# An attention and mixture-of-experts kernel: constant tables reordered, two set-up jobs moved back, due times that vary along the tiles

## The chip, the cores and the metric

One Trainium2 chip, one core of it. The metric is device time in microseconds (us) of one execution; of the kernel before, three runs are shown and their median counts. Engines are named as in the profile: PE (TensorE matmul), PEld (its weight load), DVE (VectorE), ACT (ScalarE), POOL (GpSimd), SP (SyncE, which issues most transfers).

## The reference

Attention over 8 batches, 8 heads, 576 positions of width 64, with a linear distance bias per head and a causal window of 128; then a mixture of experts on the 4608 resulting rows of width 512: each row goes to the one of 8 experts with the largest cosine similarity, passes two matrices (512 to 1024, rectified, 1024 to 512), and is scaled by its gate.

```python
scores = scale * np.matmul(q, k.transpose(0, 1, 3, 2))
bias = slopes[:, None, None] * (-np.abs(rel).astype(np.float32))[None, :, :]
mask = (rel >= 0) & (rel < window)
scores = np.where(mask, scores + bias[None], -1000000000.0)
scores = scores - np.max(scores, axis=-1, keepdims=True)
attn = np.exp(scores)
attn = attn / (np.sum(attn, axis=-1, keepdims=True) + 1e-09)
return np.matmul(attn, v).astype(np.float32)
...
logits = xn @ en.T / tau
expert_idx = np.argmax(logits, axis=1)
...
    h = np.maximum(x[mask] @ w1[e], 0.0)
    out[mask] = gate_w[mask, None] * (h @ w2[e])
```

## The kernel before, in words

**Attention** runs over 36 tiles of 128 rows. A batch has four whole tiles and a rest of 64 rows; the rests of two batches make one "pair" tile. A batch's first tile needs no previous keys. Each tile is done in two half tiles of four heads, numbered u = 0 to 71. A half tile passes these stages, each a job on one engine: scores (PE, L565), for tiles with a previous one a merge (DVE), four maxima with the bias added from `tab_full` or `tab_first` (DVE, L592), exponentials (ACT, L600), a flip, which is a transpose through the identity matrix `ident` (PE, L609), the rounded upper half of the result (ACT, L513), the remainder as lower half (DVE, L516), two masks (POOL, L647 and L660; pair tiles write them into the buffers `tails` and `spread`, which must hold zeros elsewhere), values (PE, L680 and L695), reciprocal and normalisation (DVE, L722 and L728). The values need v as an upper half (ACT, L527) and as a difference (POOL, L535, tile `vo`). A tile's result is split again (ACT L741, POOL L754), squared and summed (ACT L750), transposed by a transfer (SP, L758) and multiplied with the expert vectors (PE, L766).

**Routing** takes the tiles in groups of 8, 8, 8, 6, 4 and 2: DVE, PE, ACT and POOL find each row's expert and its place, and POOL then scatters the group's rows tile by tile to memory sorted by expert (L867, "put"). After the third group the expert with most rows is known; its weights are fetched and split, and its first 384 rows, the "head", are computed beside the last tiles.

**The experts** follow in their own plan, with PE bound by two matrix products per expert.

**The order of the work** is written by a list scheduler, `Plan`, when the kernel is built. Each job has an engine, a guessed duration, predecessors, rings of buffers that it takes, and a due time. It picks, on the engine that can start next, the job with the earliest due time among those that can start within that engine's SLACK of the first. FREE says when each engine is through with the set-up work. A due time was STEP (2500 ns) times u plus one offset per stage from `DUE`. On the chip each engine then works strictly in the order so found, and waits where the chip differs from the guesses. `early` is a start that the plan does not go below; a job with `fill` comes after all others. The scatters are spaced by SPREAD (2600 ns) and, in due time, by `gap` (6600 ns) from one to the next in a group.

**The set-up** stands ahead of the plan and runs in the order written. POOL makes `ident`, `minus`, three parts of `erow`, `ones`, `tri` (L225 to L249), then `rel_full` by iota (L285); DVE makes slopes, `wrap_full`, `tab_full` and two masks from it (L297 to L305); POOL makes `tab_first` by four selects (L312). PE multiplies `ones` with itself ten times as a warm-up (L460), then begins the scores. SP loads k and q of tiles 0 and 1, then the expert vectors (`emb`) and tau. Two jobs on POOL follow as part of the plan: `tables` (iota tables and a zero row for the scatters, L261 to L271) and `tails` (zeros in four buffers of 128x1024, L1010). The expert vectors are normalised and flipped by a chain of 15 small jobs (L490 to L504); `expert11` scales `emb` (L501) and `expert12` flips it.

## Time and profile before

| what | value |
|---|---|
| runs | 595.65, 595.83, 597.27 us; median 595.83 |
| profiled execution | 594.54 us, span 592.7 us |
| busy in the span | PE 558.4, DVE 468.8, ACT 373.3, POOL 332.7 us |
| mean granted clock of PE | 0.985 of full speed |
| weight loads (PEld) | 367.1 us |

The busy time of an engine over the whole span mixes the attention, the join and the experts, which have different limits; stretches have to be read one by one. In a timeline row the number in brackets is how long the engine stood idle before it, and what released it. [...]

### The profile page before, as it was taken

Reading aid. Unit: us, or ns where it says so; the run is one execution under the profiler, and the core shown is the slowest. Engines: PE = TensorE matmul, PEld = TensorE weight load, DVE = VectorE, ACT = ScalarE, POOL = GpSimd, SP = SyncE. Lnnn points to the kernel's source line nnn. Section 1 sums busy time; section 2 is a strip of 40 time slices with the busy share of each in tenths; the row PEclk is TensorE's granted clock in tenths of the full one; section 3 lists DMA queues with packets and bytes.
Section 4 is the critical chain, followed back from the end, with each engine's and each line's share of the span. In section 5 each row is a group of like instructions: output and inputs, shape, how many; then the busy total and the mean of one; then the engine's idle time right before and its main releaser. Section 6 shows DMA issues by size and latency. Waiting matters only on the chain. (4 is left out here: it accounts for less than half of the span.)

```text
span 592.7 us, 16519 instructions
## 1 busy us (share of the span) xinstructions
PE 558.4 (94%) x6097; PEld 367.1 (62%) x6097; DVE 468.8 (79%) x1540; ACT 373.3 (63%) x867; POOL 332.7 (56%) x445
## 2 busy tenths in 40 slices
PE   6899999999989779999999999999999999999995
PEld 3677676776767646465654764764855845754854
DVE  5799898898888778245899986798997998997670
ACT  4799999999999964134554535654744636644320
POOL 7779899999989996312617702614623352332011
PEclk9799999999999969999999999999999999999999
DMA  6589999999899597698767263446376166221001
GB/s 232 164 187 241 242 208 214 261 238 260 223 249 231 145 240 180 201 211 297 182 168 267 107 159 123 144 110 227 112 158 232 36 178 218 78 79 64 15 19 55
DMA packets 117971, 103.05 MB, mean 174 GB/s; under 512 B 85109, under 2 KB 86133, under 8 KB 117888
## 3 DMA queue, kind: packets, MB, share of 16 engines
q1 hardware_dynamic: 112048, 83.05, 55.4%
q0 software_dynamic: 5840, 18.92, 8.8%
q8 instruction: 49, 0.80, 0.6%
q14 instruction: 34, 0.28, 0.2%
HBM read 61.92 MB, written 28.12 MB: 152 GB/s over the span
## 5 line engine op out<-in xcount | busy, mean ns | idle before, releaser
L396 POOL DMA_INDIRECT out_dram<-y,ids x32 | 43.7, 1366 | 134.0 <-ACT y L1581 93.7
L600 ACT ACTIVATE pe<-sb,nm 128x128 f32<-128x128 f32 x288 | 95.3, 402 | 8.9 <-DVE nm L592 8.6
L1568 PE MATMUL ps<-w2h,hh 128*128 128x512 f16 (+1 forms) x264 | 98.4, 373 | 0.0
L1568 PE MATMUL ps<-w2l,hh 128*128 128x512 f16 (+1 forms) x264 | 98.4, 373 | 0.0
L1568 PE MATMUL ps<-w2h,hl 128*128 128x512 f16 (+1 forms) x264 | 98.4, 373 | 0.0
L1568 PEld LDWEIGHTS <-hh 128*128 128x128 f16 x528 | 51.5, 98 | 57.9 <-issue 0.8
L1581 ACT ACTIVATE y<-ps,gs 128x512 f32<-128x512 f32 (+1 forms) x28 | 19.0, 679 | 73.5 <-PE ps L1568 58.4
L565 PE MATMUL sc<-k,q 64*64 64x192 f32 (+1 forms) x1152 | 61.3, 329 | 0.0
L609 PE MATMUL ptp<-ident,pe 128*128 128x128 f32 x288 | 56.2, 297 | 4.7 <-ACT pe L600 2.1
L513 ACT ACTIVATE pq<-ptp 128x512 f16<-128x512 f32 x78 | 58.1, 748 | 3.6 <-PE ptp L609 3.4
L592 DVE CUSTOM_DVE_ANT_0 sb<-sc,tab_full 128x128 f32<-128x128 f32 x224 | 55.5, 278 | 0.0
L516 DVE SCALAR_TENSOR_TENSOR pq<-ptp,pq 128x512 f16<-128x512 f32 x66 | 49.2, 746 | 6.4 <-ACT pq L513 5.5
L609 PEld LDWEIGHTS ptp<-ident,pe 128*128 128x128 f32 x288 | 33.3, 142 | 19.5 <-ACT pe L600 14.4
L695 PE MATMUL av<-vh,mp 128*128 128x65 f16 x384 | 39.1, 196 | 5.4 <-POOL mp L647 4.9
L1568 PEld LDWEIGHTS <-hl 128*128 128x128 f16 x264 | 25.8, 98 | 29.5
L565 PEld LDWEIGHTS sc<-k,q 64*64 64x64 f32 x1152 | 36.6, 135 | 11.8 <-issue 5.7
L1350 DVE SCALAR_TENSOR_TENSOR w2l<-ws,w2h 128x1024 f16<-128x1024 f32 x28 | 33.6, 1218 | 12.6 <-ACT w2h L1352 12.5
L1363 DVE SCALAR_TENSOR_TENSOR w1l<-ws,w1h 128x512 f16<-128x512 f32 (+1 forms) x36 | 38.6, 1087 | 6.2 <-ACT w1h L1360 6.2
L1468 PEld LDWEIGHTS <-w1h 128*128 128x128 f16 x384 | 37.6, 98 | 9.5 <-issue 0.8
L867 POOL DMA_INDIRECT xs<-rows_buf,di x36 | 37.1, 1030 | 10.5 <-issue 4.2
L754 POOL TENSOR_TENSOR rows_buf<-xf,rows_buf 128x512 f16<-128x512 f32 x36 | 41.9, 1164 | 1.5 <-ACT rows_buf L741 1.0
L1496 ACT ACTIVATE hh<-pq_a 128x264 f16<-128x264 f32 (+4 forms) x48 | 19.0, 400 | 37.2 <-DVE pq_a L1486 23.5
(256 smaller groups left out, 1673.4 us busy)
## 6 DMA issues: line engine op xcount, KB each, us to landing
ws<-moe_w_dram SPq DMA_DIRECT2D x56, 512.0 KB
q<-q_dram SPq DMA_DIRECT2D x36, 256.0 KB
ldv<-v_dram SPq DMA_DIRECT2D x36, 256.0 KB
k<-k_dram SPq DMA_DIRECT2D x32, 256.0 KB
stg<-moe_w_dram SPq DMA_DIRECT2D x16, 256.0 KB
xs<-zrow SPq DMA_DIRECT2D x3, 835.2 KB
xs<-zrow SPq DMA_DIRECT2D x8, 257.0 KB
xs<-zrow SPq DMA_DIRECT2D x1, 1156.5 KB
```

The source lines that it names most:

```text
L396: ins = nc.gpsimd.indirect_dma_start(out[:, :], bass.IndirectOffsetOnAxis(ap=ids, axis=0), y, None, bounds_check=NTOK - 1, oob_is_err=False)
L513: nc.scalar.activation(hi, ps, AF.Copy, scale=scale)
L516: nc.vector.scalar_tensor_tensor(lo, ps, scale, hi, op0=ALU.mult, op1=ALU.subtract)
L565: nc.tensor.matmul(sc[T, hf, j][l * REM : (l + 1) * REM, i, c0 : c0 + (n1 - n0) * REM].rearrange("p (n c) -> p n c", c=REM), qT[T][rows, h ...
L592: nc.vector.tensor_tensor_reduce(sb_t[T, hf][:, 2 * j + i, :], sc[T, hf, j][:, i, c0 : c0 + P], tab, -QS, BIG, ALU.add, ALU.min, nm_t[T, h ...
L600: nc.scalar.activation(pr_t[T, hf][:, n, :], sb_t[T, hf][:, n, :], AF.Exp, bias=nm_t[T, hf][:, n : n + 1], scale=-1.0)
L609: nc.tensor.matmul(pt.rearrange("p (l j) c -> p l j c", j=2)[:, :, j, i * REM : (i + 1) * REM], pe[:, n, :], ident.rearrange("p (l c) -> p ...
L695: nc.tensor.matmul(o_, a_, b_, start=False, stop=(n == last), skip_group_check=True)
L754: nc.gpsimd.tensor_tensor(xx[:, DM : 2 * DM], xf_t[T], xx[:, 0:DM], op=ALU.subtract)
L1363: nc.vector.scalar_tensor_tensor(dst, src, scale, hi, op0=ALU.mult, op1=ALU.subtract)
L1468: nc.tensor.matmul(pq[key], a, b, start=(first and i == 0), stop=(i == len(jobs) - 1), skip_group_check=True)
L1568: nc.tensor.matmul(ps, x[:, ft, a * P : (a + 1) * P], w[:, ft, c], start=(which != 2 and n == 0), stop=(which != 1 and n == len(jobs) - 1) ...
```

## The change

1. Set-up order. `ones`, `eone` and `erow` are cleared or filled by DVE first. POOL begins with `rel_full`, then `ident`, then `tab_first`; the parts of `erow`, `minus` and `tri` come behind. The warm-up has 7 matmuls instead of 10.
2. Loads. Only k and q of tile 0 stand ahead of the plan; those of tile 1 are jobs of the plan, and so are the loads of `emb` and tau (`load_emb`).
3. Jobs on POOL. `tables` is due at 8 steps (20 us) instead of 2 us; the zeros of `tails` and `spread` are four jobs, due at 11 steps (27.5 us) instead of one at 4 steps (10 us), and only masks of pair tiles wait for them.
4. The first normalisation of tile 2 (u = 4) waits for `expert12`.
5. Due times. Each stage has an offset at the half tiles 0, 12, 30, 50 and 71, and in between a straight line. All are new, and with them SLACK and FREE. In thousands of ns, some of them, before and at the five knots:

| stage | before | after |
|---|---|---|
| score | -49.1 | -119.3, -71.1, -94.9, -32.8, -84.4 |
| mask | 4.9 | -124.5, -67.1, -8.4, -34.3, -76.3 |
| av | -68.0 | -114.3, -80.5, -90.3, -137.2, -52.8 |
| route | 3.6 | 3.1, -37.4, -58.0, -52.0, -81.7 |
| put | -21.9 | -198.0, -181.2, -76.4, -44.0, -123.8 |
| gap (one value) | 6.6 | -59.7 |

The two `DUE` lines and the renaming of `emb` to `emb_box["t"]` are left out of the diff.

```diff
...
@@ -51,16 +51,17 @@
 VBUFS = {"vl": 3, "v": 4}
 XBUFS = 13
 SBUFS = 2
-WARM = 10
+WARM = 7
 STG = 6
 STEP = 2500
-SLACK = {'PE': 142, 'ACT': 10, 'DVE': 0, 'POOL': 23, 'SP': 147}
+SLACK = {'PE': 141, 'ACT': 0, 'DVE': 0, 'POOL': 0, 'SP': 147}
 LAT_MOE = {"SP": 2150, "DVE-DVE": 125, "POOL-POOL": 125}
 SLACK_MOE = {"PE": 100, "ACT": 100, "DVE": 50, "POOL": 400, "SP": 300}
 LAT = {"SP": 2900, "DVE": 185, "DVE-ACT": 125, "DVE-PE": 200, "ACT": 185, "ACT-DVE": 165, "PE": 205, "POOL": 130, "DVE-DVE": 150, "POOL-POOL": 60, "ACT-ACT": 60}
-FREE = {"SP": 3000, "POOL": 7000, "DVE": 5600, "PE": 5600, "ACT": 1300}
+FREE = {"SP": 1000, "POOL": 6700, "DVE": 3300, "PE": 3300, "ACT": 1300}
 EXPERT = 9000
...
+KNOTS = [0, 12, 30, 50, 71]
...
 LAST = 3
 SPREAD = 2600
 MASK = [1230, 1650]
@@ -224,29 +225,33 @@
     aconst = early.enter_context(tc.tile_pool(name="aconst", bufs=1))
     nc.scalar.preload_act_table_set("natural_log_exp_and_others")
     ident = const.tile([P, P], F32, name="ident")
-    make_identity(nc, ident)
     minus = aconst.tile([P, P], F16, name="minus")
-    nc.gpsimd.tensor_scalar(minus, ident, -1.0 / SP_, None, op0=ALU.mult)
-    eps = np.float32(1e-9 * SP_ / SX)
-    eparts = []
-    for n in range(3):
-        part = (eps.view(np.uint32) & np.uint32(0xFFFF0000)).view(np.float32)
-        eparts.append(float(part))
-        eps = np.float32(eps - part)
     erow = aconst.tile([P, P], BF16, name="erow")
     eone = aconst.tile([P, 4], BF16, name="eone")
-    nc.vector.memset(eone, 1.0)
-    nc.gpsimd.memset(erow, 0.0)
-    for n in (2, 1, 0):
-        nc.gpsimd.affine_select(
-            erow, erow, pattern=[[0, P]], compare_op=ALU.is_gt, fill=eparts[n], base=-n, channel_multiplier=1
-        )
     tri = aconst.tile([P, P], BF16, name="tri")
     ones = aconst.tile([P, P], BF16, name="ones")
-    nc.gpsimd.memset(ones, 1.0)
-    nc.gpsimd.affine_select(
-        tri, ones, pattern=[[1, P]], compare_op=ALU.is_gt, fill=0.0, base=0, channel_multiplier=-1
-    )
+
+    def first_consts():
+        nc.vector.memset(ones, 1.0)
+        nc.vector.memset(eone, 1.0)
+        nc.vector.memset(erow, 0.0)
+
+    def later_consts():
+        eps = np.float32(1e-9 * SP_ / SX)
+        eparts = []
+        for n in range(3):
+            part = (eps.view(np.uint32) & np.uint32(0xFFFF0000)).view(np.float32)
+            eparts.append(float(part))
+            eps = np.float32(eps - part)
+        for n in (2, 1, 0):
+            nc.gpsimd.affine_select(
+                erow, erow, pattern=[[0, P]], compare_op=ALU.is_gt, fill=eparts[n], base=-n, channel_multiplier=1
+            )
+        nc.gpsimd.tensor_scalar(minus, ident, -1.0 / SP_, None, op0=ALU.mult)
+        nc.gpsimd.affine_select(
+            tri, ones, pattern=[[1, P]], compare_op=ALU.is_gt, fill=0.0, base=0, channel_multiplier=-1
+        )
+
     iota_e = const.tile([P, E], F32, name="iota_e")
     desc_e = const.tile([P, E], F32, name="desc_e")
     eoff = const.tile([P, E], F32, name="eoff")
@@ -429,15 +434,17 @@
                 loaded[T] = x = ld.tile([P, H, D], F32, tag="ldv", name=f"ldv_{T}")
                 nc.sync.dma_start(x, v[T].rearrange("p (h d) -> p h d", h=H))
 
-        for T in range(2):
-            for nm in "kq":
-                load(T, nm)
+        for nm in "kq":
+            load(0, nm)
         tmp_box["pool"] = xp
-        emb = tmp_tile("emb")[0:E]
-        nc.sync.dma_start(emb, moe_expert_emb)
         rtau = const.tile([P, 1], F32, name="rtau")
         ktau = const.tile([P, 2], F32, name="ktau")
-        nc.sync.dma_start(rtau, moe_tau.to_broadcast([P, 1]))
+        emb_box = {}
+
+        def load_emb():
+            emb_box["t"] = tmp_tile("emb")[0:E]
+            nc.sync.dma_start(emb_box["t"], moe_expert_emb)
+            nc.sync.dma_start(rtau, moe_tau.to_broadcast([P, 1]))
 
         board = banks["pool"].tile([P, 512], F32, tag="board", name="board", bufs=1)
        ...
@@ -460,9 +467,12 @@
                 nc.tensor.matmul(pt, ones, ones.unsqueeze(1).to_broadcast([P, 4, P]), start=True, stop=True)
 
         bias_rel()
+        first_consts()
+        warm(WARM)
+        make_identity(nc, ident)
         bias_table()
         first_table()
-        warm(WARM)
+        later_consts()
 
         enc = {}
 
@@ -481,14 +491,14 @@
             def flip():
                 pe_ = board[:, BK + 2 * BW : BK + 2 * BW + KT * E]
                 for kt in range(KT):
...
@@ -993,32 +1003,36 @@
             return [(f"{what}{u}{tail}", ORDER)] if u >= 0 else []
 
         def due(stage, u):
-            return STEP * u + 1000 * DUE[stage]
+            i = max(n for n, x in enumerate(KNOTS[:-1]) if x <= max(u, 0))
+            f = (u - KNOTS[i]) / (KNOTS[i + 1] - KNOTS[i])
+            return STEP * u + 1000 * (DUE[f"{stage}{i}"] * (1 - f) + DUE[f"{stage}{i + 1}"] * f)
 
         def k_tiles(T):
             pv_ = prevs(T)
             return [T] + ([] if pv_ is None else list(pv_) if isinstance(pv_, tuple) else [pv_])
 
-        for T in range(2):
+        for T in range(1):
             for n in "kq":
                 J(
-                    f"load_{n}{T}", "SP", 1100, lambda: None, due=-1e6 + T, uses=[(n, tiles[T][1] if n == "k" else T)],
+                    f"load_{n}{T}", "SP", 1, lambda: None, due=-1e6 + T, uses=[(n, tiles[T][1] if n == "k" else T)],
                     makes=[(n, (n, tiles[T][1] if n == "k" else T))] if n == "q" or not T else [],
                 )
-        J("tables", "POOL", 2500, misc_tables, due=2000)
-        J("expert_rows", "DVE", 300, expert_rows, after=["tables"], due=5000)
-        J("tails", "POOL", 1800, lambda: [nc.gpsimd.memset(x, 0.0) for x in tails + spread], due=STEP * 4, early=EXPERT)
+        J("load_emb", "SP", 900, load_emb, due=3000, early=3000)
+        J("tables", "POOL", 3000, misc_tables, due=STEP * 8)
+        J("expert_rows", "DVE", 300, expert_rows, after=["tables"], due=STEP * 9)
+        for i, x in enumerate(tails + spread):
+            J(f"tails{i}", "POOL", 890, lambda x=x: nc.gpsimd.memset(x, 0.0), due=STEP * 11 + i, early=EXPERT)
         last = None
         for i, (e, ns, f) in enumerate(expert_ops()):
             last, prev = f"expert{i}", last
-            J(last, e, ns, f, after=[prev] if prev else [], due=STEP * 6 + 100 * i, early=EXPERT)
+            J(last, e, ns, f, after=[prev, "load_emb"] if prev else ["load_emb"], due=STEP * 6 + 100 * i, early=EXPERT)
         enc_done = last
 
         for T in range(NT):
             kind, b, t = tiles[T]
             u0 = 2 * T
             pair = kind == "pair"
-            if T >= 2:
+            if T >= 1:
                 J(f"load_q{T}", "SP", 1100, lambda T=T: load(T, "q"), makes=[("q", ("q", T))], uses=[("q", T)], due=due("q", u0))
                 J(
                     f"load_k{T}", "SP", 1100, lambda T=T: load(T, "k"), makes=[("k", ("k", b))] if not t else [],
@@ -1083,7 +1097,7 @@
                     after=[f"sub{u}" if rest else f"phi{u}"], uses=[("ptp", u), ("pq", u)], due=due("plo", u),
                 )
                 J(
-                    f"mask{u}", "POOL", 0 if first else MASK[pair], lambda a=a: mask_pool(*a), after=[f"plo{u}"] + (["tails"] if pair else []),
+                    f"mask{u}", "POOL", 0 if first else MASK[pair], lambda a=a: mask_pool(*a), after=[f"plo{u}"] + [f"tails{i}" for i in range(4 * pair)],
                     makes=[] if first else [(f"tails{hf}", ("md", u))] + [("spread", ("mp", u, 0))] if pair else [("md", ("md", u)), ("mp", ("mp", u, 0))], uses=[("pq", u)], due=due("mask", u),
                 )
                 mk_ = [("pq", u)] if first else [("md", u), ("mp", u, 0)]
@@ -1097,7 +1111,7 @@
                     uses=[("av", u)], due=due("norm", u),
                 )
                 J(
-                    f"norm{u}", "DVE", 335, lambda a=a: normalize(*a), after=[f"recip{u}"] + then("norm", u - 1) * hf,
+                    f"norm{u}", "DVE", 335, lambda a=a: normalize(*a), after=[f"recip{u}"] + then("norm", u - 1) * hf + ["expert12"] * (u == 4),
                     makes=[("xf", ("xf", T))] if hf == 0 else [], uses=[("av", u), ("rs", u), ("xf", T)],
                     due=due("norm", u) + 300,
                 )
@@ -1181,7 +1195,7 @@
             for g in range(G):
                 J(
                     f"put{T0 + g}", "POOL", 1180 if gi < LAST else 1270, of(gi, 3, g), dma=750, after=[done, prev[0], f"gate{gi}_0", f"xlo{T0 + g}"] + ([(f"put{T0 + g - 1}", SPREAD)] if gi <= LAST and T0 + g else []), uses=[("gx", T0 + g)],
-                    due=due("put", u) + (1000 * DUE["gap"] if gi < LAST else 1200) * g,
+                    due=due("put", u) + (1000 * DUE["gap0"] if gi < LAST else 1200) * g,
                 )
             if gi == GP:
                 ops = [(e, ns) for e, ns, _ in head_ops({})][1:]
```

## Rows read from the trace of the kernel before

**Rows 1.** The first line of the page.

```profile
span 592.7 us, 16519 instructions
```

**Rows 2.** Table by stretch: busy us (and instructions) per engine, granted clock, DMA share, GB/s.

```profile
20.00:70.00 50.00, 47.44 (x919) 35.60 (x916) 46.30 (x252) 49.56 (x137) 40.78 (x55) 0.98 0.91 208
20.00:206.50 186.50, 170.89 (x3372) 127.95 (x3369) 163.98 (x923) 183.32 (x501) 168.56 (x228) 0.99 0.95 222
206.50:222.00 15.50, 11.21 (x138) 8.12 (x139) 11.06 (x21) 9.97 (x23) 14.27 (x18) 0.68 1.02 246
...
249.00:587.00 338.00, 336.12 (x2283) 208.95 (x2281) 267.72 (x477) 161.43 (x301) 120.78 (x127) 1.00 0.47 143
```

**Rows 3.** ACT's waits from 20 to 212 us: total, times, longest.

```profile
ACT pe L600 <- DVE nm L592: 1.8, 3, 1.1
```

**Rows 4.** Timeline of all engines from 0 to 9 us: start, duration, engine, line.

```profile
0.78 0.20 POOL masks.py:197 MEMSET ident<- 128x128 f32 x1 [0.29 <-POOLq L1958]
...
0.85 0.06 DVE L238 MEMSET eone<- 128x4 bf16 x1 [0.85 <-PEq L1958]
...
2.65 0.21 POOL L246 MEMSET ones<- 128x128 bf16 x1
...
2.91 4.45 PE L460 MATMUL pt_warm<-ones 128*128 128x512 bf16 x10 [2.91 <-POOL ones L246]
...
3.31 0.75 POOL L285 IOTA rel_full<- 64x256 f32 x2
...
4.09 0.29 DVE L298 TENSOR_SCALAR wrap_full<-rel_full 128x256 f32<-128x256 f32 x1 [2.81 <-POOL rel_full L285]
...
5.57 2.75 POOL L312 TENSOR_SCALAR_AFFINE_SELECT tab_first<-tab_full 64x512 bf16<-64x512 bf16 x4 [1.51 <-DVE tab_full L303]
...
7.29 1.52 PE L565 MATMUL sc<-k,q 64*64 64x128 f32 x32
...
8.88 2.45 ACT L600 ACTIVATE pe<-sb,nm 128x128 f32<-128x128 f32 x8 [6.81 <-DVE nm L592]
```

**Rows 5.** Table by stretch, columns as in group 2, while the first loads arrive.

```profile
1.50:3.50 2.00, 0.59 (x2) 0.28 (x3) 0.00 (x0) 0.57 (x1) 1.84 (x7) 1.00 0.76 249
```

**Rows 6.** Timeline of PE from 11 to 30 us: two score jobs.

```profile
18.64 1.56 PE L565 MATMUL sc<-k,q 64*64 64x192 f32 x16
...
23.73 0.88 PE L565 MATMUL sc<-k,q 64*64 64x192 f32 x16
```

**Rows 7.** Timeline of all engines from 8 to 22 us: the stall.

```profile
8.59 0.18 POOL L261 IOTA iota_e<- 128x8 f32 x1
...
11.49 1.84 POOL L1010 MEMSET tails<- 128x1024 f16 x2
11.82 0.61 ACT L527 ACTIVATE vh<-ldv 128x512 f16<-128x512 f32 x1
...
13.27 1.84 POOL L1010 MEMSET spread<- 128x1024 f16 x2
...
15.19 2.21 POOL L535 TENSOR_TENSOR vo<-ldv,vh 128x512 f16<-128x512 f32 x2
...
16.36 0.21 PE L695 MATMUL av<-vo,pq 128*128 128x64 f16 x1 [3.39 <-POOL vo L535]
...
18.75 0.74 ACT L513 ACTIVATE pq<-ptp 128x512 f16<-128x512 f32 x1 [2.87 <-PE ptp L609]
...
21.24 0.64 POOL L647 TENSOR_SCALAR_AFFINE_SELECT md<-pq 128x512 f32<-128x512 f32 x1 [3.85 <-DVE pq L516]
```

**Rows 8.** Timeline of DVE from 28 to 34 us.

```profile
30.15 0.40 DVE L728 TENSOR_TENSOR xf<-av,rs 128x256 f32<-128x256 f32 x1
...
31.16 0.46 DVE L501 TENSOR_SCALAR emb<-emb,er 8x512 f32<-8x512 f32 x1
```

**Rows 9.** Timeline of POOL from 140 to 190 us: two scatters.

```profile
141.18 0.99 POOL L867 DMA_INDIRECT xs<-rows_buf,di  x1 [0.17 <-issue]
...
145.79 0.98 POOL L867 DMA_INDIRECT xs<-rows_buf,di  x1 [0.16 <-PE ptp L609]
```

More of the change, by code (lines that the diff above doesn't have):

```diff
@@ L483, in flip @@
                 for kt in range(KT):
[L484 removed]
+                    nc.tensor.transpose(pe_[:, kt * E : (kt + 1) * E], emb_box["t"][:, kt * P : (kt + 1) * P], ident[:E, :E])
                 z["pv"] = pe_.rearrange("p (a e) -> p a e", a=KT)
@@ L490, in expert_ops @@
                 ("DVE", 90, lambda: V.tensor_scalar(ktau[:, 0:1], rtau, 0.5 * SX * SEN, None, op0=ALU.mult)),
-                ("ACT", 120, lambda: nc.scalar.activation(xp.tile([P, DM], F16, tag="junk", name="junk_e", bufs=1)[:E], emb, AF.Square, accum_out=c1("en2"))),
+                ("ACT", 120, lambda: nc.scalar.activation(xp.tile([P, DM], F16, tag="junk", name="junk_e", bufs=1)[:E], emb_box["t"], AF.Square, accum_out=c1("en2"))),
                 ("DVE", 90, lambda: V.tensor_scalar(ktau[:, 1:2], rtau, 1e-6 * SX * SEN, None, op0=ALU.mult)),
@@ L500, in expert_ops @@
                 ("DVE", 90, lambda: V.reciprocal(c1("er"), c1("ez"))),
-                ("DVE", 90, lambda: V.tensor_scalar(emb, emb, c1("er"), None, op0=ALU.mult)),
+                ("DVE", 90, lambda: V.tensor_scalar(emb_box["t"], emb_box["t"], c1("er"), None, op0=ALU.mult)),
                 ("PE", 60, flip),
```

3 lines of the change are left out of this document (1 added, 2 removed).

## The prediction

> **What bounds the kernel now.** I read the header of the page, the table by stretch, ACT's waits, then the timeline of the first 25 us. The profiled execution has a span of 592.7 us [rows 1]; its own time is 594.54 us, so 1.84 us lie around the span. It is 1.29 us under the median of the runs, 595.83. The sum below is made against 594.54, and 1.29 is added at its end.
>
> The table by stretch [rows 2] shows two kernels one after the other. From 20 to 206.5 us, attention, ACT is busy 183.3 of 186.5 us, more than PE (170.9) or POOL (168.6), so ACT sets the pace. From 249 to 587 us, the experts, PE is busy 336.1 of 338 us. Between them, from 206.5 to 222, PE is busy only 11.2 of 15.5 us and its mean granted clock is 0.68. Inside the attention ACT loses almost nothing: its largest group of waits there comes to 1.8 us [rows 3]. So an edit is worth something if ACT starts earlier, if ACT stops less in the first 20 us, or if the hole at the join closes; whatever ACT ends earlier with, PE's full stretch can begin earlier with.
>
> **The start.** ACT's first exponential begins at 8.88 us. It follows the first scores on PE, which begin at 7.29, directly behind ten warm-up matmuls that run from 2.91 to 7.36 (445 ns each); these wait for `ones`, which POOL writes at 2.65 to 2.86. Beside that runs the table path: POOL's iota starts at 3.31, DVE's wrap at 4.09, POOL's `tab_first` at 5.57, and that ends at 8.32 [rows 4]. Both paths end just before 8.6, so bias tables first would bring almost nothing alone, nor would fewer warm-ups alone; the diff does both. Three steps:
> - Warm-up. `ones` moves to DVE as its first instruction. DVE's first now runs at 0.85; the moved one has the size of POOL's (0.21 us), so PE begins at about 1.1. Seven matmuls at 0.445 take 3.1, so scores begin at 4.2 instead of 7.29: 3.1 us earlier.
> - Tables. The iota can start where `ident` begins now, 0.78, and takes 0.75. From iota start to DVE's wrap are 0.78, from wrap to the first select 1.48, and the four selects take 2.75 [rows 4]: 0.78 + 0.78 + 1.48 + 2.75 = 5.8. The first exponential, 1.59 behind the scores as now, comes at 5.8, and needs only the first half of the selects (done at 4.4). The tables no longer bind. `ident`, `erow`, `minus` and `tri` follow on POOL, 1.7 to 2 us of work; flips and values come later than these, so I price them at nothing. Gone cover would cost at most those 2 us.
> - Data. Tile 0's k and q (128 + 256 KB) are the first two transfers now as then. From 1.5 to 3.5 us 249 GB/s land, 498 KB in all [rows 5], over 384 KB, so they are there by 4.2. Moving tile 1's k and q and the two small loads (embedding, tau) behind takes four issues off SP's queue ahead of the first v, and nothing early waits for them.
>
> Value: **-3.1**. If the data lands 1.3 us later than I read, -1.8; more than -3.1 is excluded by PE's order.
>
> [...] A score job of 16 matmuls takes 1.56 us where the granted clock is 0.5 and 0.88 where it is 1.0 [rows 6]; for the smaller first tile, two thirds of the columns, that is 0.45 us more. [...] Most of it is covered by the four first maxima on DVE. Between 0 and +0.45 I take **+0.2**.
>
> [...]
>
> **The stall at 16 us.** POOL writes zeros to `tails` and `spread` from 11.49 to 15.11, and the scatter tables before that from 8.59. The first value halves on ACT end at 12.43, but POOL's difference `vo` starts only at 15.19. PE's values wait 3.39 us for it, at 16.36; PE works in order, so the next flips wait behind them and ACT stands for 2.87 us until 18.75 [rows 7]. With both jobs moved back (due at 20 and 27.5 us of the plan), `vo` starts about 2.7 us earlier against its value halves. What is late next is the 1.1 us of `vo` itself, leaving PE some 0.7 of its 3.39, which ACT has work to cover. Value **-2.7**, bounds -2.87 and -1.5 (if a memset, about 0.9, still falls ahead of it, and some of `vo` shows). PE's low clock after that stop (the 1.56 us score job at 18.64) goes as well; ACT bounds there, so nothing is counted.
>
> **The work that is moved.** 2.9 us of tables (8.59 to 11.49) and 3.6 us of memsets, 6.5 in all, land on POOL between 20 and 50 us. POOL is busy 40.8 of 50 us between 20 and 70 [rows 2]: 9.2 idle, of which 3.85 at 21.24 belong to the stall [rows 7] and 5.4 remain, besides POOL's own earlier freedom. Masks queued behind one memset of 0.9 wait at most that, and ACT has queued tiles. Between 0 and +6.5 I take **+0.4**.
>
> **The new wait.** Tile 2's first normalisation now waits for the embedding's flip. Before, it ran at 30.15 and the embedding's scaling only at 31.16 to 31.62 [rows 8], so in the old order the wait would be about 1.5 us and a flip on PE; on DVE the maxima would queue behind it, and ACT behind those. The plan can pull the chain forward. Between 0 and +1.8 I take **+0.3**.
>
> **The new due times** have no row. They leave the instructions and their count alone, so ACT's total in the attention stays. A gain there is bounded by ACT's idle 3.2 us from 20 to 206.5 plus PE's idle 4.3 us at the join [rows 2]; a loss by the bursts below. I take 0, nearest to ACT's almost full row.
>
> Sum: -3.1 + 0.2 - 2.7 + 0.4 + 0.3 = -4.9. 594.54 - 4.9 = 589.6 for an execution like the profiled one; with 1.29 the median is **590.9 us**.
>
> **Rivals.**
> 1. *The scatters come in bursts; slower.* Before, a group's scatter on POOL came every 4.6 us (141.18, 145.79) at 0.99 + 0.17 us [rows 9], because `gap` put each 6.6 us later. Now `gap0` is -59.7, and only the 2.6 us of SPREAD keep them apart. ACT needs (206.5 - 8.9) / 36 = 5.49 us per tile. POOL without scatters (20 to 70 us, 82% busy) needs 4.48 of that; with one each 2.6 us, 2.45 more: 6.93. It falls behind 1.44 us per tile, 5.5 us over the 3.8 tiles of a burst of 8. If the masks run two half tiles ahead (5.5 us), nothing stalls; if one (2.75), 2.7 us stall in each of the first three groups, 8.2 us, giving 599.1. It decides below a lead of 3.9 us (5.5 - 4.9 / 3). For it: POOL is over 90% busy through most of the attention. Against it: the plan knows what a scatter costs POOL, and can leave it waiting.
> 2. *POOL takes the front's gain back.* Only a third of the 6.5 us moved finds POOL idle, and 4.4 us show as late masks: 595.3, no change. For: the remaining 5.4 us of idleness are under 6.5. Against: POOL has 18 us idle up to 206.5.
> 3. *The join closes too.* The masks of the last tiles are pulled ahead and PE's 4.3 us idle go: 586.6. For: the due times may now differ at the end from those at the start. Against: the values, and so PE, wait there for POOL, which is busy 14.3 of 15.5 us [rows 2].
>
> **How the numbers follow.** The forecast gets 0.62, with a range of its own from 588.5 (the best ends, some of the join) to 593.5 (data late, the moved work at +2). Bursts 0.12, POOL's taking back 0.16, the join 0.10. The range, 586.6 to 596.5, holds the forecast, the second rival, and half of the third; it leaves out the bursts and the deeper half of the join. Under 0.3%, 1.8 us, a measurement of this kernel can't tell a difference from no change. Faster by more: 0.62 + 0.10 = 0.72. Within: 0.16. Slower: 0.12.
>
> **What would show it.** Right: warm-ups start at about 1.1 us, the first scores at 4.2, ACT's first exponential at 5.8; no wait of ACT on a flip of over 1 us in the first 20; the granted clock does not fall there; memsets of `tails` stand beyond 20 us; from 20 us on ACT is full, and PE's last matmul ends near 582 instead of 587. Step by step wrong: scores later than 5 (data, not warm-ups, was the limit); ACT waiting for maxima near tile 2's normalisation; ACT idle over 5 us in 70 to 200 with masks late behind scatters (bursts); POOL late in 30 to 70 (taking back). If ACT ends some 5 us earlier but PE's full stretch does not begin earlier, the join is what I have misread, and the prediction falls with it.

## The result, and the profile after

The changed kernel is slower: 601.24 us median (597.54 to 606.56, 8 runs) against 595.83 (594.98 to 598.12, 8 runs), a ratio of 1.0078 with a 95% interval of 1.0051 to 1.0106. Here and below, a ratio compares runs of two kernels on one chip and leaves out runs more than 1.5% above the fastest of their kernel, so it can differ from the quotient of two medians. The prediction was 590.9 in a range of 586.6 to 596.5. The profiled execution took 600.81 us, 6.27 more than that of before.

The first line of the page and the table by stretch of the changed kernel, with the columns of [rows 2], answer to [rows 1, 2]:

```profile
span 599.0 us, 16515 instructions
```

```profile
20.00:70.00 50.00, 45.58 (x903) 34.62 (x904) 45.05 (x239) 48.38 (x132) 41.61 (x55) 0.97 0.88 210
20.00:206.50 186.50, 168.38 (x3292) 127.15 (x3292) 163.71 (x902) 180.75 (x490) 169.56 (x226) 0.97 0.96 228
206.50:222.00 15.50, 14.09 (x182) 9.44 (x181) 10.73 (x32) 11.76 (x29) 12.80 (x20) 0.89 0.80 193
249.00:587.00 338.00, 332.41 (x2230) 205.17 (x2231) 269.36 (x476) 160.18 (x299) 121.11 (x125) 0.99 0.48 142
```

ACT is 2.6 us less busy in the attention than before; PE is 2.9 us busier at the join, at a granted clock of 0.89 instead of 0.68, but 3.7 us less busy among the experts. So the loss that reaches the end stands behind 249 us, where the prediction had changed nothing. Some of ACT's head start is gone before that, though. ACT's busy time over the first 200 us, of the kernel before, of the changed kernel, and of a run told below that has the new set-up with the old due times:

```profile
0.00:200.00 200.00, 179.58 (x3408) 132.12 (x3408) 169.16 (x957) 186.36 (x505) 176.28 (x264) 0.98 0.93 223
```

```profile
0.00:200.00 200.00, 177.41 (x3353) 131.39 (x3353) 174.05 (x957) 188.24 (x508) 180.28 (x267) 0.97 0.94 231
```

```profile
0.00:200.00 200.00, 180.67 (x3448) 132.88 (x3448) 175.29 (x985) 189.42 (x514) 178.94 (x270) 0.99 0.93 226
```

ACT (the fourth pair) is ahead of the kernel before by 1.88 us of work in the changed kernel and by 3.06 with the new set-up alone.

The start came out as foreseen. From the timeline of the first 19 us of the changed kernel, answering to [rows 4, 7]:

```profile
0.88 0.17 DVE L235 MEMSET ones<- 128x128 bf16 x1 [0.88 <-PEq L1972]
...
1.10 3.17 PE L467 MATMUL pt_warm<-ones 128*128 128x512 bf16 x7 [1.10 <-DVE ones L235]
...
4.31 1.24 PE L575 MATMUL sc<-k,q 64*64 64x128 f32 x32
...
5.61 2.45 ACT L610 ACTIVATE pe<-sb,nm 128x128 f32<-128x128 f32 x8 [3.54 <-DVE nm L602]
...
8.30 0.18 POOL L266 IOTA iota_e<- 128x8 f32 x1
...
11.27 2.21 POOL L545 TENSOR_TENSOR vo<-ldv,vh 128x512 f16<-128x512 f32 x2
...
12.45 0.19 PE L705 MATMUL av<-vo,pq 128*128 128x64 f16 x1 [2.29 <-POOL vo L545]
...
13.42 1.84 POOL L1024 MEMSET tails<- 128x1024 f16 x2
13.45 0.76 ACT L523 ACTIVATE pq<-ptp 128x512 f16<-128x512 f32 x1 [0.75 <-PE ptp L619]
```

Warm-ups at 1.10 us, scores at 4.31, the first exponential at 5.61 instead of 8.88; `vo` at 11.27 instead of 15.19, and ACT's stop behind it 0.75 us instead of 2.87. But `tables` still stands ahead of `vo` (8.30 to 11.27), and three of the four memsets of zeros come directly behind it, from 13.42 to 16.15, not beyond 20 us.

Where the time went is seen in PE's waits from 245 us to the end, of the changed kernel (total, times, longest):

```profile
PE ps L1533 <- DMA xT<-xs: 5.4, 1, 5.4
PE pq_b L1482 <- DVE u L1500: 3.0, 2, 1.7
```

Before, the three waits there were 0.8, 0.4 and 0.3 us. The first wait is for the first expert's remaining rows (`xT`), which follow the last scatter; the second is for a part of the third expert's hidden layer that DVE makes (`u`). POOL's timeline of the changed kernel shows why the rows are late:

```profile
222.97 0.95 POOL L877 DMA_INDIRECT xs<-rows_buf,di  x1 [1.95 <-DVE gs_head L967]
...
228.03 0.96 POOL L877 DMA_INDIRECT xs<-rows_buf,di  x1 [0.19 <-issue]
...
229.38 1.16 POOL L764 TENSOR_TENSOR rows_buf<-xf,rows_buf 128x512 f16<-128x512 f32 x1
```

The remainder of the last tile (L764), whose upper half ACT has at 221.5 us, stands behind five scatters of earlier tiles, since the offset of their due times has gone from -21.9 us to between -44.0 and -123.8 there. Its logits, its group's routing and the last scatter wait for it. Before, that remainder ran at 223.47, ahead of these scatters. After the wait PE is slow for a while; the table by stretch of the changed kernel:

```profile
249.00:252.00 3.00, 0.56 (x3) 0.41 (x4) 1.23 (x1) 0.00 (x0) 0.28 (x2) 0.73 0.64 168
252.00:256.00 4.00, 4.00 (x19) 2.42 (x18) 0.46 (x1) 0.41 (x1) 0.52 (x3) 0.50 0.19 69
256.00:260.00 4.00, 4.00 (x29) 2.98 (x28) 0.91 (x2) 0.82 (x2) 0.00 (x0) 0.85 0.99 297
```

At a granted clock of 0.50 of full speed PE does 19 matmuls in the four microseconds in which it does 29 at 0.85.

The milestones below are read from the timelines, in us; the last four columns are runs told further down. Each column is one profiled execution, of 594.54, 600.81, 595.51, 595.44, 593.49 and 592.40 us; that of "split first" lies 4.4 us under its run's median.

| milestone | before | changed | set-up alone | split first | weights first | before, POOL relieved |
|---|---|---|---|---|---|---|
| ACT's last exponential ends | 205.26 | 207.33 | 200.82 | 209.30 | 208.80 | 204.07 |
| `x_head` (the head's rows) issued on SP | 203.32 | 199.35 | 203.46 | 200.43 | 198.75 | 201.71 |
| last product with v ends | 219.16 | 218.54 | 219.30 | 219.13 | 218.74 | 216.38 |
| first expert's other rows on PE | 250.37 | 251.44 | 249.72 | 247.73 | 248.58 | 247.60 |
| second expert, hidden layer | 272.50 | 276.38 | 271.85 | 269.86 | 270.71 | 269.73 |
| second expert, output layer | 301.07 | 304.39 | 300.41 | 301.73 | 298.71 | 298.20 |
| third expert, hidden layer | 326.97 | 330.29 | 326.31 | 327.62 | 324.61 | 324.10 |
| third expert, output layer | 347.14 | 353.35 | 348.08 | 347.93 | 345.79 | 344.79 |
| last matmul ends | 586.75 | 593.03 | 587.58 | 587.50 | 585.44 | 584.43 |

Changed against before: rows late +1.07; first expert (24.94 instead of 22.13 us, part of it at half clock) +2.81; second expert -0.56; third expert's hidden layer (23.06 instead of 20.17) +2.89. That is 6.21 of the 6.28 us at the last matmul. ACT's last exponential ends 2.07 us later in the changed kernel, though the first began 3.27 us earlier; the last product with v does not follow it.

### The profile page after: what moved, and what is told of

Same layout as the page of the kernel before. It is cut to its first block, busy times and chain, and to the rows that moved or that the text cites. A ratio compares the mean times of both kernels' runs of the same rounds, so it can differ in the third digit from the quotient of the medians.

```text
span 599.0 us, 16515 instructions
## 1 busy us (share of the span) xinstructions
PE 559.7 (93%) x6094; PEld 367.9 (61%) x6094; DVE 471.0 (79%) x1542; ACT 374.0 (62%) x867; POOL 334.8 (56%) x445
## 5 line engine op out<-in xcount | busy, mean ns | idle before, releaser
L619 PE MATMUL ptp<-ident,pe 128*128 128x128 f32 x288 | 57.9, 302 | 6.4 <-ACT pe L610 2.9
L526 DVE SCALAR_TENSOR_TENSOR pq<-ptp,pq 128x512 f16<-128x512 f32 x66 | 50.4, 763 | 7.5 <-ACT pq L523 6.1
L1533 PE MATMUL ps<-xT,w1h 128*128 128x288 f16 (+2 forms) x192 | 42.4, 315 | 5.4 <-DMA xT<-xs 5.4
L1377 DVE SCALAR_TENSOR_TENSOR w1l<-ws,w1h 128x512 f16<-128x512 f32 (+1 forms) x36 | 41.0, 1150 | 6.6 <-ACT w1h L1374 6.6
L764 POOL TENSOR_TENSOR rows_buf<-xf,rows_buf 128x512 f16<-128x512 f32 x36 | 42.9, 1194 | 5.3 <-ACT rows_buf L751 4.5
```

Source lines behind the costliest of these rows:

```text
L526: nc.vector.scalar_tensor_tensor(lo, ps, scale, hi, op0=ALU.mult, op1=ALU.subtract)
L619: nc.tensor.matmul(pt.rearrange("p (l j) c -> p l j c", j=2)[:, :, j, i * REM : (i + 1) * REM], pe[:, n, :], ident.rearrange("p (l c) -> p ...
L764: nc.gpsimd.tensor_tensor(xx[:, DM : 2 * DM], xf_t[T], xx[:, 0:DM], op=ALU.subtract)
L1377: nc.vector.scalar_tensor_tensor(dst, src, scale, hi, op0=ALU.mult, op1=ALU.subtract)
L1533: nc.tensor.matmul(ps[:, :w], a[:, kt, fs], xx[:, b + kt, c0 : c0 + w], start=(n == 0), stop=(n == len(jobs) - 1))
```

## The experiments

Ratios are to the kernel before on the same chip, with 95% intervals. Line numbers shift by one to three between kernels.

**The halves of the change.** The changed kernel once more, then the set-up with the old due times, then the old set-up with the new ones.

```diff
 # set-up alone: the changed kernel with the old lines
-KNOTS = [0, 12, 30, 50, 71]
-DUE = {'av0': -114.3, ...
+DUE = {'av': -68.0, ...
-SLACK = {'PE': 141, 'ACT': 0, 'DVE': 0, 'POOL': 0, 'SP': 147}
+SLACK = {'PE': 142, 'ACT': 10, 'DVE': 0, 'POOL': 23, 'SP': 147}
...
```

> The changed kernel unaltered, for a second profile and times on the same chip as the three others. All theories: 600 to 602. Theory L: again a wait of 4 us or more for the rows after the head, and half clock behind it. Rival E: again about 3 us of PE's waiting for DVE near 334 to 342; if it is not there this time, it is chance and no part of the change.

> The changed kernel with the old due times, gap and SLACK: set-up order, 7 warm-ups, moved loads and POOL jobs alone. Theory L: the front's gain is kept and the last remainder stands ahead of the scatters as in the kernel before, so the experts begin 2 to 4 us earlier than there: 592.5 (591 to 594.5). Rival F (front): the early set-up itself costs later, by POOL's moved work or the new wait of tile 2: 597 or more. Rival E: experts start early but end late: 596 to 600.

> The kernel before with the new due times, gap and SLACK alone, its set-up kept. In its order the last remainder stands ahead of the scatters. Theory L: the due times cost through that one place; without it they cost little: 596 to 599. Rival D: the new due times are worse through the whole attention (POOL's bursts, ACT's waits), so attention ends some us later: 601 or more.

Changed again: 603.62 us, 1.0152 [1.0120, 1.0183]; PE waits 6.6 us for the rows and 2.9 for `u`, so both belong to the order and not to one execution. Set-up alone: 595.93, 1.0028 [1.0011, 1.0045]. New due times on the old set-up: 609.97, 1.0256 [1.0229, 1.0282]. So the due times cost the time, and the set-up by itself brings none (it costs some 0.3%), although ACT's last exponential ends 4.44 us earlier with it. On the old set-up the rival came true: the attention itself ends late there, the last product with v at 231.62 us. PE's waits from 206 to 222 us of the set-up alone, in its timeline:

```profile
208.59 0.24 PE L704 MATMUL av<-vh,tails 128*128 128x65 f16 x1 [2.42 <-POOL tails L669]
...
210.91 0.21 PE L704 MATMUL av<-vo,tails 128*128 128x64 f16 x1 [2.08 <-POOL vo L544]
```

Two waits for POOL, as before (1.67 and 2.10 us at 209.48 and 211.82). Its last product with v is where it was.

**The late remainder.** The changed kernel, with the scatters of tiles 29 to 33 ordered behind the last tile's remainder.

```diff
-... if gi <= LAST and T0 + g else []), uses=[("gx", T0 + g)],
+... if gi <= LAST and T0 + g else []) + ([f"xlo{NT - 1}"] if 29 <= T0 + g < NT - 2 else []), uses=[("gx", T0 + g)],
```

> The changed kernel, and only this: the scatters of tiles 29 to 33 may not stand ahead of the last tile's remainder (the subtract into rows_buf) on POOL. Theory L (late rows): in the changed kernel POOL does that remainder behind five scatters, at 229.4 us though its input is there at 221.5; so the last transpose, the last two scatters and the first expert's rows come late, PE has finished the head at 246.0 and stands 5.4 us until 251.4, and works at half clock until about 257. Then here the remainder runs before 223 us, PE's wait for the rows shrinks to 1.5 us or less, the clock stays at 1.0, and the median is 594.5 (592.5 to 597). Rival E (experts): the loss lies in the expert stage, where the profile shows 3 us of PE waiting for DVE at 334 to 342; then the time stays at 599 or more.

599.80 us, 1.0041 [1.0011, 1.0072], spread from 591.8 to 603.4; by the ratio some 597 on that chip, where the changed kernel itself gave 1.0152 [1.0120, 1.0183]. So the late remainder is worth some 1.1% (0.4% if the first comparison, 1.0078, is taken); the median spoke for the rival, the waits for theory L. In its profile, of an execution of 595.44 us, the rows' wait and the half clock went, and the first expert started 3.7 us earlier. The second expert's hidden layer then took 31.9 us instead of 28.0. PE's waits from 250 us on, and SP's transposes of the second expert's rows, of this run:

```profile
PE ps L1533 <- ACT w1h L1366: 2.0, 1, 2.0
PE ps L1533 <- DVE w1l L1364: 1.4, 2, 0.8
```

```profile
251.13 11.49 SPq L1300 DMA_TRANSPOSE xT<-xs  x1
...
264.85 0.35 SPq L1346 DMA_DIRECT2D ws<-moe_w_dram  x1
...
266.67 0.36 SPq L1346 DMA_DIRECT2D ws<-moe_w_dram  x1
```

The kernel before, same view:

```profile
253.34 9.16 SPq L1286 DMA_TRANSPOSE xT<-xs  x1
```

Begun 2.2 us earlier, the transposes end at the same time (262.6 and 262.5 us), and the last two w1 loads behind them come no earlier (264.85 and 266.67 us; before, 264.74 and 266.57). An early start does not always lengthen them: on the kernel before with POOL relieved, told below, they begin at 250.64 us and take 9.11.

**The second expert's weights.** Its four w1 loads ahead of its rows: on the split-first run, on the kernel before, and on the changed kernel alone.

```diff
-J(f"get{w_}_{s}_{c}", "SP", 1456, ..., due=d, ...
+J(f"get{w_}_{s}_{c}", "SP", 1456, ..., due=d - 24000 * (p == 1 and w_ == 1), ...
```

> The changed kernel with the last tile's remainder ahead of the late scatters (as in the split-first run) and, besides, the second expert's four w1 loads issued on SP ahead of that expert's transposed rows instead of two of them behind. Theory A (in the split-first run the second expert's hidden layer took 31.9 us instead of 28.6 because its last w1 loads stood on SP behind the rows, whose transposes end at 262.6 us whether they start at 251 or 253): the waits of PE for w1h and w1l (2.0 and 1.4 us) go, the second expert's output layer starts at about 298.5 us instead of 301.7, and the time falls by 2 to 4 us under the split-first run (599.8). Rival B (the DMA engines are full there, so that the order of loads changes nothing): the wait moves to the rows of the second expert (PE waits 2 to 4 us for xT), the output layer starts at 301 to 302 us, the time stays within 1 us.

> The kernel before with only the second expert's four w1 loads ahead of its rows on SP, as in the weights-first run. Theory A (in the kernel before the second expert's weights are hidden: PE waits 0.4 us for them): the second expert's output layer starts within 0.8 us of 301.07, the time stays within 1 us of 594.5, and the gain of the weights-first run (593.5 against 599.8 split-first) needs the change's earlier start. Rival B (the edit is a gain by itself): the output layer starts at 298 to 299 us and the time falls by 2 us or more.

> The changed kernel with only the second expert's w1 loads first, the last tile's remainder left behind the late scatters. Theory A (the late remainder costs 3 to 4 us by itself, whatever the weights do): the rows of the first expert are waited for by 5 to 7 us again, the first expert runs at half clock, and the time is 599 to 603, 6 to 9 us above the run with both edits (593.5). Rival B (the order of the weights is what the changed kernel lacked, the remainder is covered): 593 to 596.

With both edits: 593.49 us, 0.9950 [0.9919, 0.9981], faster than either kernel; no wait of PE for w1 is left, and the output layer starts at 298.71. On the kernel before the edit costs time: 599.37, 1.0070 [1.0046, 1.0093], which neither theory had. On the changed kernel alone: 599.66, 1.0071 [1.0047, 1.0094]. PE's longest wait behind 245 us, first of the run on the kernel before, then of that on the changed kernel:

```profile
PE ps L1519 <- DVE y_head L975: 5.5, 1, 5.5
```

```profile
PE ps L1533 <- DMA xT<-xs: 8.2, 1, 8.2
```

In the first, DVE's part of the head's output (`y_head`) is late. ACT and DVE of that run show why:

```profile
250.80 1.06 ACT L1352 ACTIVATE w1h<-ws 128x1024 f16<-128x1024 f32 x1 [5.26 <-DMA ws<-moe_w_dram]
```

```profile
251.89 1.23 DVE L1350 SCALAR_TENSOR_TENSOR w1l<-ws,w1h 128x1024 f16<-128x1024 f32 x1 [5.67 <-ACT w1h L1352]
253.03 0.74 DVE L975 TENSOR_SCALAR y_head<-ps_head,gs_head 128x512 f32<-128x512 f32 x1
```

A weight split that the edit brought forward in DVE's order waits there, by way of ACT, for its load, and `y_head` stands behind it; in the kernel before only one such split, at 246.53, stands ahead of it, and `y_head` ran at 249.56. The second shows the late remainder again. On the changed kernel the weights first alone bring nothing clear (1.0071, against 1.0078 and 1.0152 for the kernel itself); behind the split first they bring it from 1.0041 to 0.9950. The second limit shows only when the first is mended.

**What paces the join.** First, the last six low parts of v moved from POOL to DVE, in the set-up alone and in the kernel before.

```diff
-nc.gpsimd.tensor_tensor(lo, loaded[T], ...
+(nc.vector if T >= 30 else nc.gpsimd).tensor_tensor(lo, loaded[T], ...
```

> The set-up alone, with the low parts of v of the last six tiles (30 to 35) subtracted on DVE instead of POOL. Six rows of 1.1 to 1.5 us, some 7 us, leave POOL between 176 and 211 us. Theory A (POOL, not ACT, paces the end of attention: it has no wait over 0.5 us there, while PE waits 2.4 us for tails and 2.1 us for vo): the last product with v on PE ends at 215 to 217 us instead of 219.3, the two waits of PE fall under 1 us, the first expert starts 2 to 4 us earlier than 249.7, and the time falls by 2 to 4 us below the set-up alone (595.9). Rival B (ACT paces it, as the prediction said): the last product stays within 1 us of 219.3, the time within 1 us of 595.9. Rival C (something behind the join, the weights of the second expert, sets the end): the first expert starts 2 to 4 us earlier, but its second expert's weights are waited for by as much, and the time stays within 1 us.

> The kernel before with the low parts of v of the last six tiles on DVE instead of POOL, the same edit as in the first of these runs. Theory A (POOL paces the end of attention in the kernel before too): the last product with v ends 2 to 4 us earlier than 219.2 us, the first expert starts 2 to 3 us earlier than 250.4, and the time falls by 1.5 to 3 us from 594.5, less what the second expert's weights take back. Rival B (ACT paces it, whose last exp ends at 205.3 us): the last product moves by less than 1 us, and the time by less than 1 us; DVE's extra 4 us may even cost 1 to 2 us.

599.22, 1.0032 [0.9998, 1.0066] and 600.04, 1.0070 [1.0038, 1.0102]: neither gained, and in the second the last product with v came 3.7 us later, at 222.85, against both theories. POOL's waits from 170 to 226 us of the second run:

```profile
POOL md L647 <- ACT pq L513: 5.3, 2, 3.4
POOL xs L867 <- DVE xf L728: 1.7, 1, 1.7
```

DVE had some 6 us more to do, ACT's last exponential ended 4.4 us later (209.62), and POOL, relieved, waits for both. So this told nothing of POOL by itself. Next, the staged loads behind `x_head` cut to half:

```diff
-nc.sync.dma_start(x, hd["jobs"][i][0])
+h_ = DM // 2 if i >= STG else DM
+nc.sync.dma_start(x[:, 0:h_], hd["jobs"][i][0][:, 0:h_])
...
```

> The set-up alone, with the last ten of the first expert's sixteen staged weight loads cut to half their columns (the half that came stands in for the other, so the expert outputs of the first expert are others). In the set-up alone these ten take 11.2 us of SP from 208.96 to 220.2, three transposed tiles stand behind them, and ACT waits 3.0 us for them. Theory A (SP and the transfers behind x_head pace the join): the ten end by 216 us, ACT's wait for stg goes, the first expert's other rows start 2 to 4 us earlier than 249.7 us. Rival B (POOL's last remainder at 222.6 us and the start of the head at 213 us pace it, the loads are hidden): the first expert's other rows start within 1 us of 249.7, and the time stays within 1.5 us of 595.9.

595.92, 1.0007 [0.9985, 1.0029], rows at 248.78: rival B, those loads are hidden. Last, POOL relieved without loading another engine:

```diff
+w_ = 64 if 24 <= T < 35 else DM
-nc.gpsimd.tensor_tensor(xx[:, DM : 2 * DM], xf_t[T], xx[:, 0:DM], op=ALU.subtract)
+nc.gpsimd.tensor_tensor(xx[:, DM : DM + w_], xf_t[T][:, 0:w_], xx[:, 0:w_], op=ALU.subtract)
```

> The set-up alone, with the remainders of the routed rows of tiles 24 to 34 on POOL cut from 512 to 64 columns (the other columns keep what was there, so the rows' low halves are others): eleven operations of 1.16 us fall to some 0.2, about 10 us of POOL between 155 and 219 us, and no other engine gets work for it. Theory A (POOL, without a wait over 0.5 us from 170 to 222 us, paces the end of attention in the set-up alone; ACT, whose last exp ends at 200.8, does not): the last product with v ends at 214 to 217 us instead of 219.3, PE's waits for tails (2.4) and vo (2.1 us) fall under 1 us, the granted clock from 206 to 222 us rises from 0.67 to over 0.85, the first expert's other rows start at 245 to 248 us instead of 249.7. The time falls by 1 to 4 us under 595.9, less if the second expert's weights take it back (output layer after 300 us). Rival B (x_head's transposed rows, 203.46 us, pace it): x_head stays at 203 to 204 us, and the first expert's other rows start within 1 us of 249.7.

> The kernel before with the same cut of eleven remainders on POOL. Theory A (POOL paces the end of attention in the kernel before as well): the last product with v ends 2 to 4 us before 219.2 us, PE's waits for tails (1.7) and vo (2.1 us) fall under 1 us, the first expert's other rows start at 247 to 249 us instead of 250.4, and the time falls by 1 to 3 us under 594.5 to 595. Rival B (ACT, whose last exp ends at 205.3 us): last product and time within 1 us.

On the kernel before: 594.02, 0.9972 [0.9957, 0.9988]; last product at 216.38, 2.8 us earlier, rows 2.8 us earlier, last matmul 2.3 us earlier. On the set-up alone: 594.51, 0.9985 [0.9969, 1.0001], that is 0.43% under its unrelieved self by the ratios; last product 1.4 us earlier. Waits of POOL in the second case, from 170 to 222 us:

```profile
POOL rz L844 <- ACT junk L759: 5.2, 2, 5.0
POOL md L656 <- DVE rs L731: 1.9, 1, 1.9
```

POOL's longest waits there were these in the kernel before and in the set-up alone:

```profile
POOL xs L867 <- issue: 1.3, 8, 0.2
```

```profile
POOL rz L847 <- DVE rz L846: 0.5, 1, 0.5
```

Relieved, it waits itself, and DVE's and ACT's busy time there stays within 1.2 us of what it was. So POOL paced the end of attention in both kernels, with the next limit close behind: some 9 us less of its work (eleven operations of 0.3 instead of 1.16 us) bring 0.28% and 0.43%. The milestones are of single executions and scatter: the kernel before with the weights first, whose attention is unedited, ended its last product at 217.96, so that of the two moves only the 2.8 us stand clear. Two expectations failed in the set-up alone: PE's waits for `vo` and `tails` did not shrink, only moved earlier, and the granted clock from 206 to 222 us came to 0.71, not over 0.85.

**Only the early scatters.** The set-up alone with the new due times of four stages (logit, route, put, gap) and the remainder first; then with the weights first as well.

> The set-up alone plus only those new due times that bring the scatters of rows (logit, route, put, the gap between puts), with the last tile's remainder ahead of the late scatters; every other due time as before. Theory A (the set-up's head start was lost because the first expert's transposed rows, x_head, wait on SP for a scatter that POOL issues at 200 us in either case, 203.46 us against 203.32; what the new due times give is a scatter that comes earlier): x_head is issued at 198 to 201 us, the head of the first expert starts on PE at 209 to 211 us instead of 213.15, the first expert's other rows at 246 to 248 us instead of 249.7; the second expert's weights then take it back as in the split-first run (output layer at 300.5 to 302 us), so that the time stays within 2 us of the set-up alone (595.9). Rival B (x_head's place is not what holds the join: the staged weights behind it or POOL are): x_head earlier, but the first expert's other rows start no earlier than 249 us.

> The first of these runs with the second expert's w1 loads first as well. Theory A: both gains add: the first expert's other rows at 246 to 248 us, the second expert's output layer at 297 to 299 us, the time 2 to 4 us under the set-up alone (595.9), 592 to 594, about that of the weights-first run (593.5) or a little below, since ACT's last exp ends earlier here. Rival B (DMA is full when ACT runs ahead): x_head or the staged weights come no earlier, and the time stays at 595 to 597.

602.93, 1.0127 [1.0088, 1.0165] and 600.70, 1.0098 [1.0065, 1.0132]: both theories fell. `x_head` left at 206.59 and 207.57, later than with all new due times on the new set-up (198.75 to 203.44), and PE waited 3.2 and 3.1 us for it. Here these four stages did not bring it forward without the rest.

**DVE beside POOL.** Weight subtractions on POOL cut, first for the third expert (`p == 2`), then for the fourth, as shown.

```diff
+h_ = 8 if p == 3 and n != 3 else FH
-nc.gpsimd.tensor_tensor(o, x, y, op=ALU.subtract)
+nc.gpsimd.tensor_tensor(o[:, 0:h_], x[:, 0:h_], y[:, 0:h_], op=ALU.subtract)
```

> The changed kernel with three of the four subtractions of weights on POOL for the third expert cut to 8 columns of 512 (the sums of that expert are left out, so its output is another). Theory A (in the changed kernel the third expert's hidden layer takes 23.1 us instead of 20.2 because DVE's splits run beside POOL's subtractions of two operands and are stretched, 4.24 us for one of 1024 columns that takes 1.21 otherwise, so that DVE's parts come 3 us late): no split on DVE in that stretch above 2 us, PE's wait of 3 us for u goes, the hidden layer takes 20.2 us, the time falls by 2.5 to 3.5 us below the changed kernel's (601 to 603.6). Rival B (DVE is late because its inputs are, from DMA or PE): splits may be short, but the hidden layer stays at 22.5 to 23.5 us and the time within 1 us.

> The changed kernel with three of the four weight subtractions on POOL cut to 8 columns of 512 for the fourth expert, whose weights are prepared while the third expert's hidden layer runs (330 to 353 us); the earlier run cut the third expert's, which are done by 308 us. The fourth expert's sums are left out, so its output is another. Theory A (DVE's splits are stretched beside these subtractions): in that stretch no split of 512 or 1024 columns takes over 2.2 us except beside the one subtraction left (1.28 us each), PE's wait for u falls from 3.0 us to under 1.2, the hidden layer takes 20.0 to 20.6 us instead of 23.1, and the time falls by 2 to 3.5 us under the changed kernel's (1.0078 to 1.015 of the kernel before, so 1.003 to 1.011). Rival B (something else stretches DVE there): splits of 3.3 to 4.2 us remain, and the hidden layer takes 22 us or more.

The first cut missed: beside the third expert's hidden layer run the subtractions for the fourth, and splits of 3.92 and 3.33 us remained (600.61, 1.0075 [1.0045, 1.0105]); yet the wait for `u` fell from 3.0 to 0.9 us and the hidden layer to 20.82. The second hit its subtractions. DVE and POOL of the changed kernel, then DVE of the second run:

```profile
329.42 4.24 DVE L1377 SCALAR_TENSOR_TENSOR w1l<-ws,w1h 128x1024 f16<-128x1024 f32 x1 [0.25 <-ACT w1h L1374]
330.06 1.28 POOL L1414 TENSOR_TENSOR ws<-ws,ws 128x512 f32<-128x512 f32 x1
331.28 1.29 POOL L1414 TENSOR_TENSOR t<-ws,ws 128x512 f32<-128x512 f32 x1
...
336.14 3.33 DVE L1377 SCALAR_TENSOR_TENSOR wxl<-t,wxh 128x512 f16<-128x512 f32 x1
...
336.41 2.50 POOL L1414 TENSOR_TENSOR ws<-ws 128x512 f32<-128x512 f32 x2
```

```profile
334.25 2.32 DVE L1377 SCALAR_TENSOR_TENSOR w1l<-ws,w1h 128x1024 f16<-128x1024 f32 x1 [0.25 <-issue]
...
339.06 0.68 DVE L1377 SCALAR_TENSOR_TENSOR wxl<-t,wxh 128x512 f16<-128x512 f32 x1
```

Where the subtractions are gone, 3.33 becomes 0.68 us; the wait for `u` is gone, and the hidden layer takes 19.46 us instead of 23.06. The whole (600.46, 1.0094 [1.0070, 1.0117]) can't show it: the changed kernel's own two comparisons lie at 1.0078 and 1.0152, and this execution began its first expert at 257.3 us.

Nor does it show that the subtractions make the loss. The changed kernel with the weights first, no subtraction cut, also has no wait for `u` and a hidden layer of 19.46 us; its first expert began late too, at 254.78, and during that layer its splits ran apart from the subtractions. The first cut left the stretched splits and took most of the wait. That a split is longer beside the subtractions is shown; that this, and not how far DVE is ahead of PE, costs the third expert's 2.9 us stays open.

## Why the prediction was wrong

**"The start", -3.1 + 0.2: right.** The first exponential came 3.27 us earlier. No run shows the +0.2: the two score jobs took 1.24 us instead of 1.52, and the granted clock reads 1.00 under the warm-ups and these jobs in both kernels ([rows 5]; of the changed kernel, from 1.10 to 5.56 us). The warm-ups take 445 ns each [rows 4] even so, where matmuls of 512 columns at a granted clock of 1.00 follow one another every 0.216 us in the head (243.69 to 245.63 us of the changed kernel); why, no run shows.

**"The stall at 16 us", -2.7: the reason right, the size not.** `vo` came 3.92 us earlier: 3.70 because the zeros now stand behind it, 0.22 because `tables` ended earlier. But ACT's one stop of 2.87 us became three of 0.57, 0.75 and 0.39, together 1.71: the term measured -1.2, under its own bound of -1.5, since ACT then waits for DVE's maxima as well. `tables` stayed, and most of the zeros moved by one place. A due time is no earliest start: the planner fills POOL's free time with what is ready. So **"the work that is moved"** was wrong about the place; and of the 3.85 us of idleness that it took off, only 1.2 lie behind 20 us, so that 8.0 us and not 5.4 were left. For it and **"the new wait"** together 0.7 was foreseen; from 20 to 70 us ACT was 0.97 us less busy in the set-up alone (48.59 instead of 49.56), by another way: it waited 1.41 us, at 27.10, for PE's flip of the expert vectors. In the changed kernel that wait is not there, and the normalisations ran unheld, at 28.01 and 29.96.

Up to the end of ACT's work, then, -4.9 was foreseen, and the set-up alone has -4.44 at its last exponential. That this is near is partly luck of order: by 200 us ACT is ahead by 3.06 us of work, and the rest comes from a half of v (0.62 us, L536) that now stands behind the last exponential and other changes of place. In the changed kernel ACT is 1.88 us ahead.

**"What bounds the kernel now": the step that failed first.** The sentence was that "whatever ACT ends earlier with, PE's full stretch can begin earlier with". It can't: with ACT's end at 200.8, 205.3 or 209.3 us the last product with v ends at 219.1 to 219.3 (over the ten executions of these orders of the attention with ACT's end from 200.8 to 209.3 it lies between 217.96 and 219.70, without following it; only where ACT ended at 212.24, in the run without the fourth expert's subtractions, did it come at 222.41). I had read the share of ACT over the whole attention and POOL's 168.6 of 186.5 us as slack. But half of POOL's idle time lies before 70 us; from 170 us on it has no wait over 0.2 us, and its 14.27 of 15.5 us at the join [rows 2] I used only against a rival. The relieved runs show POOL as the pacer, with another limit at most 2.8 us behind it. The prediction named this outcome as the one with which it falls.

**"The new due times", 0: the step that turned the sign.** They "have no row", and I gave them no place behind ACT. They brought a better join (no stop of PE for POOL there, granted clock 0.89) and three losses: the late remainder with the half clock behind it, the second expert's w1 loads, which show only when the first is mended, and 2.9 us in the third expert's hidden layer, whose cause stays open. Measured against the set-up alone on the same chip, they cost 1.2% (1.0152 against 1.0028).

**The rivals.** A burst did cost, but not by 2.7 us in each of three groups, nor through `gap`, which the last groups don't use: one burst of five, at the join, held one job of 1.16 us. From 70 to 200 us ACT's idle time rose only from 2.7 to 4.1 us (5.1 in the second profile), where three bursts would have added 8.2. POOL did take the front's gain back, at the end and not between 30 and 70 us; that was 595.3 in the prediction, and the set-up alone gave 595.93. The join did close, by 2.9 of its 4.3 us, and what it gave was lost behind it.

## What to carry to other kernels

A share of busy time over a whole stage names the bound of its middle; what a head start was worth here was decided by the engine that had no gap near the end of the stage. Where an order is written by a planner, look first for the one late job that much waits for, and at what has been given an earlier due time on its engine. Mending one limit of a chain may show nothing while another stands before it: here the weights first gave 1.0071 by themselves, where the changed kernel had 1.0078 and 1.0152, and 0.9950 behind an edit that alone gave 1.0041.

## What the runs showed of the hardware

A split on DVE of 1024 columns took 4.24 us beside POOL's subtractions and 1.21 to 1.22 in stretches without; one of 512 columns 3.33 and 0.68. Both read two operands, and so do POOL's subtractions (`w1l<-ws,w1h` and `ws<-ws,ws` in the rows above). In length, 3.33 us is about the 2.50 of the POOL work that began beside it and 0.68 of its own. By its recorded start this split began first, at 336.14 against 336.41, and it ended last, at 339.47 against 338.91. What makes it longer beside them, no run shows.

I had not expected either that after PE's wait of 5.4 us the granted clock was 0.50 from 252 to 256 us, while PE worked without a gap, so that 1.07 us of lateness cost another 2.81 in the first expert. SP's transposes of the second expert's rows took 11.49 us in the split-first run and 10.80 in the weights-first run, against 9.16 in the kernel before, 8.74 in the changed kernel and 9.11 in the kernel before with POOL relieved. What lengthens them was not tried.
